# Fetching q and k as bfloat16 in runs of 18 tokens, in a kernel of block-causal attention followed by a hash-routed MoE

## The chip, the core and the metric

The kernel runs on one core of one Trainium2 chip. The metric is the device time of one execution in microseconds; before the change its median over three runs is 338.91 us (338.58 to 340.65). A profile shows where that time goes; its span, from the first to the last instruction, is 334.5 us.

The core has five engines that run side by side and wait for each other through semaphores: TensorE (PE in the profile; its weight loads are PEld), VectorE (DVE), ScalarE (ACT), GpSimd (POOL, called Pool in the text) and SyncE (SP), which here only starts transfers. Transfers between the chip's memory (HBM) and the on-chip memory (SBUF) run on 16 DMA engines, whoever starts them. TensorE writes its results to a small memory of its own, PSUM, from which VectorE or ScalarE must copy them.

## What is computed

```python
# attention: batch 8, heads 8, 576 tokens, head size 64
scores = q @ k.T / sqrt(64)                 # per batch and head
scores = where(pos_i // 64 >= pos_j // 64, scores, -1e9)   # causal by blocks of 64 tokens
x      = softmax(scores) @ v                # -> x: 4608 tokens x 512
# routing: each token goes to one of 8 experts
expert = token_ids * 2654435761 % 8
# expert e, on its tokens only
out[tokens of e] = relu(x[tokens of e] @ w1[e]) @ w2[e]    # 512 -> 1024 -> 512
```

All inputs and the output are float32 in HBM.

## The kernel before

The kernel works on *pairs* of two heads of one batch: 32 pairs, `g = 4 * b + pr`. For each pair it needs q and k with the head size on the partitions, so it fetches them with the tokens on the partitions, casts them to bfloat16 and transposes them on TensorE. `m` is the head within a pair; the two heads lie in the two halves of the partitions.

```python
    def load_qk(b, h0=0, h1=H, rest=True, main=True, engs=None):
        # float32, tokens 4p..4p+3 of a head on partition p (q), 2p, 2p+1 of each half (k);
        # the last 64 tokens in transfers of their own
        ...
            if main and w == 0:
                eng.dma_start(
                    t[:, 4 * h0 : 4 * h1, :].rearrange("p (h c) d -> p h (c d)", c=4),
                    src[b, h0:h1, 0:512, :].rearrange("h (p c) d -> p h (c d)", c=4),
                )
        ...

    def cast_qk(b, which, r0=0, r1=NP, rest=True):
        ...
            nc.vector.tensor_copy(           # float32 -> bfloat16, two pairs per call
                dst[:, 8 * r0 : 8 * r1, :].rearrange("p (r c m) d -> p r m c d", c=4, m=2),
                src[:, 8 * r0 : 8 * r1, :].rearrange("p (r m c) d -> p r m c d", c=4, m=2),
            )
        if rest:
            nc.gpsimd.tensor_copy(dst[:, 32:36, :], src[:, 32:36, :])

    def T_pair(g):                            # eight 128x128 transposes, one copy
        ...
        tp = psT.tile([P, 2, 512], BF16, name="tp", tag="tp")     # psT has two buffers
        for w in range(2):
            for c in range(4):
                ...
                nc.tensor.transpose(out=o, in_=..., identity=identbf[:])   # L236
        nc.vector.tensor_copy(qk[:, pr, :, 0:512], tp[:])                  # L241
    # T_rest(b): four transposes and two small copies (L211, L217) for the last 64 tokens
```

The scores of a pair are made in three chunks. The block mask is added on TensorE by a product of two small constant tiles. ScalarE takes the exponential into `pt`, the product with v follows two pairs later, and VectorE divides by the row sums (`norm`).

```python
    def mm_pair(b, pr, ps, o0, kt, q0, n, first=False):                    # L248
        for m in range(2):
            rows = slice(64 * m, 64 * m + 64)
            nc.tensor.matmul(ps[:, m, o0 : o0 + n],
                lhsT=qk[rows, pr, 1, 128 * kt : 128 * kt + 128],
                rhs=qk[rows, pr, 0, q0 : q0 + n], start=first, stop=False)
    # mm_c: the same in 64x64 tiles (L260); mm_mask: the mask product (L270)
    # S_chunk: mm_pair, mm_mask, then nc.scalar.activation(..., ACT.Exp)   # L294
    # PV(g, m): O = pt.T @ v, 15 matmuls (L331, L336); psO has one buffer
    # norm(g): reciprocal (L348) and two multiplications into xs (L351)
    # cast_v: v to bfloat16, on Pool but for the first batch (L188 to L199)

    def write_x(b):
        eng = nc.sync if b < BA - 1 else nc.gpsimd        # BA = 6
        for t in range(NT):                               # queries are held permuted
            r0 = S * b + P * t
            eng.dma_start(
                x_dram[r0 : r0 + P, :].rearrange("(j c) d -> c j d", c=4), xs[:, t, :])
        eng.dma_start(x_dram[S * b + 512 : S * b + S, :], xs[0:64, NT, :])
```

The routing is worked out beside the attention: `place_a` and `place_b` turn token numbers into lists of rows, one batch of tokens per two pairs. The MoE gathers rows of `x_dram` by these lists (`gather_x`, an indirect transfer on Pool, L567), transposes them, and runs two matmul stages per expert. Tokens of batches 0 to 5 are gathered early (tiles 0 to GA), those of batches 6 and 7 when the attention is over.

```python
    for g in range(NPAIRS + 2):
        b, pr = divmod(g, NP)
        ... S_chunk(g, 0); PV(g - 2, 0); S_chunk(g, 1); PV(g - 2, 1); norm(g - 2); S_chunk(g, 2)
        ... T_pair(g + 2); cast_qk(b + 1, ...); T_rest(b + 1) at pr == 2
        ... place_a at steps 5, 7, .. 19; place_b at steps 8, 10, .. 22
        ... cast_v for pair g + 3
        if pr == 1 and b >= 1:
            write_x(b - 1)
        if pr == (1 if b == 0 else 0) and b + 2 < B:
            load_qk(b + 2)
            load_v(b + 2)
        if g in (25, 26):
            load_w1(g - 25)            # 2 MB of float32, cast to bfloat16 in the transfer, Pool
        if g == 29:
            load_w2(0)
        if g in (27, 28):
            gather_x(g - 27, 0, GA)
    ...
    gather_x(0, GA, G)
    gather_x(1, GA, G)
    load_w2(1)
    for e in range(2):
        transpose_x(e, 0, GA)          # L683, L684
        stage_a_part(e, 0, GA)         # x @ w1 and relu: L715, L719
    ... then the late tiles, stage_b(0) (h @ w2: L729, L734, L736) and experts 2 to 7
```

Of the kernel before, what the change touches and what calls it, by code (L numbers as in the profile page):

```python
# [7 lines left out]
ALU = mybir.AluOpType  # L8
# [11 lines left out]

B, H, S, D = 8, 8, 576, 64
E, DM, FF = 8, 512, 1024
N = B * S
NT = 4
# [13 lines left out]
def kernel(  # L38
# [62 lines left out]
    def load_qk(b, h0=0, h1=H, rest=True, main=True, engs=None):  # L101
        if b not in loaded:
            loaded[b] = [ld.tile([P, 36, D], F32, name="qf", tag="qf"),
                         ld.tile([P, 36, D], F32, name="kf", tag="kf"), None]
        for w, src in ((0, q), (1, k)):
            t = loaded[b][w]
            eng = engs[w] if engs else nc.sync
            if main and w == 0:
                eng.dma_start(
                    t[:, 4 * h0 : 4 * h1, :].rearrange("p (h c) d -> p h (c d)", c=4),  # L110
                    src[b, h0:h1, 0:512, :].rearrange("h (p c) d -> p h (c d)", c=4),
                )
            elif main:
                for r in range(2):
                    eng.dma_start(
                        t[:, 4 * h0 : 4 * h1, :].rearrange(
                            "p (h r c) d -> p h r (c d)", r=2, c=2)[:, :, r],
                        src[b, h0:h1, 256 * r : 256 * r + 256, :].rearrange("h (p c) d -> p h (c d)", c=2),
                    )
            if rest:  # L120
                for g in range(2):
                    eng.dma_start(
                        t[64 * g : 64 * g + 64, 32:36, :],
                        src[b, 4 * g : 4 * g + 4, 512:576, :].rearrange("h r d -> r h d"),
                    )

    def load_v(b):
# [7 lines left out]
        for m in range(2):  # L135
            nc.sync.dma_start(
                vf[64 * m : 64 * m + 64, 32:36, :],
                v[b, :, 512:576, :].rearrange("(r m) s d -> m s r d", m=2)[m],
            )
        loaded[b][2] = vf  # L140

    casted = {}
# [24 lines left out]
    def cast_qk(b, which, r0=0, r1=NP, rest=True):  # L167
        src = loaded[b][which]
        cb = casted.setdefault(b, {})
        if which not in cb:  # L170
            cb[which] = att.tile([P, 36, D], BF16, name="qb" if which == 0 else "kb",
                                 tag="qb" if which == 0 else "kb")
        dst = cb[which]
        if r1 > r0:
            nc.vector.tensor_copy(
                dst[:, 8 * r0 : 8 * r1, :].rearrange("p (r c m) d -> p r m c d", c=4, m=2),
                src[:, 8 * r0 : 8 * r1, :].rearrange("p (r m c) d -> p r m c d", c=4, m=2),
            )
        if rest:
            nc.gpsimd.tensor_copy(dst[:, 32:36, :], src[:, 32:36, :])  # L180

    def cast_v(b, pr):
        vf = loaded[b][2]
        vx, v4 = vexts[b % 2]
        hs = slice(2 * pr, 2 * pr + 2)
        vm = vf[:, 0:32, :].rearrange("p (h s) d -> p h s d", h=H)
        eng = nc.vector if b == 0 and pr < 2 else nc.gpsimd
        eng.tensor_copy(vx[:, hs, 0:4, 0:D], vm[:, hs])  # L188
        if pr % 2:
            return  # L190
        hs = slice(2 * pr, 2 * pr + 4)
        nc.gpsimd.tensor_copy(vx[0:64, hs, 4:6, 0:D], vm[0:64, hs, 0::2, :])
        nc.gpsimd.tensor_copy(vx[64:128, hs, 4:6, 0:D], vm[0:64, hs, 1::2, :])

    def cast_v4(b):
        vf = loaded[b][2]
# [8 lines left out]
    def T_rest(b):  # L205
        qk = qkTs[b]
        tp = psT.tile([P, 8, P], BF16, name="tp", tag="tp")
        for w in range(2):
            src = casted[b][w]
            for x in range(2):  # L210
                nc.tensor.transpose(  # L211
                    out=tp[:, 2 * w + x, :],
                    in_=src[:, 32 + 2 * x : 34 + 2 * x, :].rearrange("p a d -> p (a d)"),
                    identity=identbf[:],
                )
        for w in range(2):
            nc.vector.tensor_copy(  # L217
                qk[:, :, w, 512:576].rearrange("p (g x) r -> p x g r", g=2),
                tp[:, 2 * w : 2 * w + 2, :].rearrange("p x (g r) -> p x g r", g=2),
            )  # L220

    def T_pair(g):
        b, pr = divmod(g, NP)
        if pr == 0:
            qkTs[b] = att.tile([P, NP, 2, S], BF16, name="qkT", tag="qkT")
        qk = qkTs[b]
        tp = psT.tile([P, 2, 512], BF16, name="tp", tag="tp")
        for w in range(2):
            src = casted[b][w]
            for c in range(4):  # L230
                s0 = (pr * 4 + c) * 2
                if w == 0:
                    o = tp[:, 0, :].rearrange("p (i c j) -> p c i j", i=4, c=4)[:, c]
                else:
                    o = tp[:, 1, 128 * c : 128 * c + 128]
                nc.tensor.transpose(  # L236
                    out=o,
# [610 lines left out]
```

## Time and profile before

| Engine | busy us | share of the span | instructions |
|---|---|---|---|
| TensorE (PE) | 276.5 | 83% | 3247 |
| TensorE weight loads (PEld) | 198.3 | 59% | 3247 |
| VectorE (DVE) | 152.5 | 46% | 342 |
| ScalarE (ACT) | 142.5 | 43% | 169 |
| Pool (POOL) | 183.4 | 55% | 265 |

| DMA queue | packets | MB | share of 16 engines |
|---|---|---|---|
| started by Pool (software) | 9248 | 32.73 | 41.1% |
| started by SyncE (hardware) | 55104 | 30.12 | 33.7% |
| started by ScalarE (hardware) | 2656 | 1.18 | 1.4% |

Busy times are sums over the whole span, and the phases of this kernel have different limits, so the totals decide nothing by themselves. TensorE's matmuls are pipelined and their ends are modelled, so a TensorE that shows as busy need not be working at its peak. Read the timeline to see which engine waits for which: an instruction that had to wait carries the idle time before it and the releaser, in brackets. The profile also states the granted TensorE clock, as a part of full speed; its mean here is 0.951.

### The profile page before, as it was taken

What the parts mean: (1) busy time and instruction counts of PE and PEld (TensorE: products, weight loads), DVE (VectorE), ACT (ScalarE), POOL (GpSimd) and SP (SyncE); (2) the same over time, 40 slices, a digit from 0 to 9 for tenths busy, and PEclk for the clock granted to TensorE, in tenths of its full rate; (3) what the DMA queues carried; (4) which work ended last, traced back from release to release, by engine and by line L of the source; (5) the groups of instructions that cost most, each with busy time, mean ns of one, the idle gap of its engine ahead of it and who ended that gap; (6) DMA issues with size and microseconds to landing.
All of it is one profiled execution on the core that took longest, in us unless ns stands there. A gap on an engine that the chain in (4) does not pass through costs nothing. (4 is left out here: it accounts for less than half of the span.)

```text
span 334.5 us, 7914 instructions
## 1 busy us (share of the span) xinstructions
PE 276.5 (83%) x3247; PEld 198.3 (59%) x3247; DVE 152.5 (46%) x342; ACT 142.5 (43%) x169; POOL 183.4 (55%) x265
## 2 busy tenths in 40 slices
PE   1559898989799899458589899799897996999990
PEld 0337676767577676347476594665745845759430
DVE  6487899888878775221011413033141130240430
ACT  1337888779687978304322050330501402406000
POOL 2185867687966529682487517447175075051451
PEclk9999999999989999959869999999999898999996
DMA  7999997979897975969189998677786586537231
GB/s 195 283 290 282 261 289 203 262 199 285 203 297 203 294 197 123 205 182 184 55 179 231 180 232 221 177 138 229 151 174 187 111 177 187 109 121 148 94 135 45
DMA packets 67044, 64.54 MB, mean 193 GB/s; under 512 B 17218, under 2 KB 61060, under 8 KB 64960
## 3 DMA queue, kind: packets, MB, share of 16 engines
q0 software_dynamic: 9248, 32.73, 41.1%
q1 hardware_dynamic: 55104, 30.12, 33.7%
q10 hardware_dynamic: 2656, 1.18, 1.4%
q8 instruction: 26, 0.43, 0.5%
q14 instruction: 10, 0.08, 0.1%
HBM read 67.15 MB, written 15.20 MB: 246 GB/s over the span
## 5 line engine op out<-in xcount | busy, mean ns | idle before, releaser
L294 ACT ACTIVATE pt<-ps 128x1024 bf16<-128x1024 f32 x96 | 94.2, 1023 | 34.4 <-PE ps L270 34.2
L701 ACT ACTIVATE hT<-hp 128x640 bf16<-128x640 f32 x48 | 33.6, 704 | 95.4 <-PE hp L696 78.6
L729 PE MATMUL yp<-w2b,hT 128*128 128x512 bf16 x320 | 70.2, 379 | 0.0
L696 PE MATMUL hp<-xT,w1b 128*128 128x320 bf16 x384 | 57.4, 309 | 9.1 <-ACT hT L701 8.2
L736 POOL DMA_INDIRECT out_dram<-ysb,perm x40 | 39.8, 995 | 38.6 <-DVE ysb L734 30.0
L696 PEld LDWEIGHTS <-w1b 128*128 128x128 bf16 x384 | 52.9, 145 | 13.5 <-issue 10.2
L567 POOL DMA_INDIRECT xg<-x_dram,perm x40 | 40.8, 1020 | 23.6 <-issue 12.9
L734 DVE COPY ysb<-yp 128x512 f32<-128x512 f32 x40 | 27.7, 692 | 55.9 <-PE yp L729 49.7
L729 PEld LDWEIGHTS <-hT 128*128 128x128 bf16 x320 | 31.1, 98 | 36.2
L684 DVE COPY xT<-tpx 128x512 bf16<-128x512 bf16 x40 | 15.6, 421 | 77.4 <-PE tpx L683 75.6
L331 PE MATMUL O<-vx,pt 128*128 128x65 bf16 x896 | 41.0, 199 | 6.7 <-DVE xs L351 5.4
L331 PEld LDWEIGHTS <-pt 128*128 128x128 bf16 x896 | 33.4, 101 | 10.2 <-issue 5.2
L248 PE MATMUL ps<-qkT 64*128 64x64 bf16 (+2 forms) x384 | 36.2, 269 | 3.0 <-ACT pt L294 2.6
L351 DVE TENSOR_TENSOR xs<-O,rs 128x320 bf16<-128x320 f32 x64 | 28.4, 486 | 1.1
L270 PE MATMUL ps<-maskq,maskk 64*128 64x64 bf16 (+1 forms) x256 | 28.1, 213 | 0.0
L188 POOL CAST vx<-vf 128x512 bf16<-128x512 f32 x30 | 21.1, 707 | 9.2 <-DMA vf<-in_v_dram 5.5
L719 ACT ACTIVATE hT<-hp 128x768 bf16<-128x768 f32 (+1 forms) x16 | 11.3, 704 | 31.7 <-PE hp L715 29.9
L241 DVE COPY qkT<-tp 128x1024 bf16<-128x1024 bf16 x32 | 22.0, 687 | 5.3 <-PE tp L236 4.6
L715 PE MATMUL hp<-xT,w1b 128*128 128x384 bf16 (+1 forms) x128 | 21.9, 338 | 2.3 <-DVE xT L684 2.3
L555 POOL DMA_DIRECT2D w1b<-in_moe_w_dram x8 | 4.8, 596 | 33.7 <-PE tpx L683 33.7
L683 PE MATMUL tpx<-identbf,xg 128*128 128x128 bf16 x160 | 14.7, 229 | 10.3 <-DMA xg<-x_dram,perm 6.6
L715 PEld LDWEIGHTS <-w1b 128*128 128x128 bf16 x128 | 17.4, 149 | 6.5 <-issue 2.9
(120 smaller groups left out, 289.6 us busy)
## 6 DMA issues: line engine op xcount, KB each, us to landing
vf<-in_v_dram SPq DMA_DIRECT2D x16, 512.0 KB, 5.9
w1b<-in_moe_w_dram POOLq DMA_DIRECT2D x8, 1024.0 KB
w2b<-in_moe_w_dram POOLq DMA_DIRECT2D x8, 1024.0 KB
qf<-in_q_dram SPq DMA_DIRECT2D x7, 1024.0 KB, 8.4
kf<-in_k_dram SPq DMA_DIRECT2D x14, 512.0 KB, 7.2
x_dram<-xs SPq DMA_DIRECT2D x20, 128.0 KB
x_dram<-xs POOLq DMA_DIRECT2D x12, 128.0 KB
qf<-in_q_dram SPq DMA_DIRECT2D x16, 64.0 KB, 6.3
```

Source lines behind the costliest of these rows:

```text
L248: nc.tensor.matmul(ps[:, m, o0 : o0 + n], lhsT=qk[rows, pr, 1, 128 * kt : 128 * kt + 128], rhs=qk[rows, pr, 0, q0 : q0 + n], start=first, ...
L270: nc.tensor.matmul(ps[:, m, o0 : o0 + 128 * n].rearrange("p (t h j) -> p t h j", h=2, j=16)[:, :, 0, :], lhsT=maskk[rows, c, :], rhs=maskq ...
L294: nc.scalar.activation(ptv[:, :, 512 * ch : 512 * ch + 512], ps[:], ACT.Exp, scale=SCALE)
L331: nc.tensor.matmul(O[:, t, :], lhsT=pt[:, m * PTW + o0 : m * PTW + o0 + 128], rhs=vx[:, h, i, :], start=(n == 0), stop=(n == t),)
L351: nc.vector.tensor_tensor(out=xs[:, :, 0:DM].rearrange("p t (d h k) -> p h t d k", d=4, h=H)[:, h], in0=O[:, m, :, 0:D].rearrange("p t (k ...
L567: nc.gpsimd.indirect_dma_start(out=xgs[g % (2 * G)][:], out_offset=None, in_=x_dram[0:n, :], in_offset=bass.IndirectOffsetOnAxis(ap=perm3[ ...
L696: nc.tensor.matmul(hp[:, t, 0:HC], lhsT=w1b[:, db, ft::NFT], rhs=xT[:, db, t * HC : (t + 1) * HC], start=(db == 0), stop=(db == NKT - 1),)
L701: nc.scalar.activation(hT[:, ft, :].rearrange("p (t n) -> p t n", t=2), hp[:, :, 0:HC], ACT.Relu)
L715: nc.tensor.matmul(hp[:, ft - f0, 0 : P * (t1 - t0)], lhsT=w1b[:, db, ft::NFT], rhs=xT[:, db, c], start=(db == 0), stop=(db == NKT - 1),)
L729: nc.tensor.matmul(yp[:], lhsT=hT[:, ft, tt * P : (tt + 1) * P], rhs=w2b[:, ft, :], start=(ft == 0), stop=(ft == NFT - 1),)
L734: nc.vector.tensor_copy(ysb[:], yp[:])
L736: ins = nc.gpsimd.indirect_dma_start(out=out[:, :], out_offset=bass.IndirectOffsetOnAxis(ap=perm3[:, gg : gg + 1], axis=0), in_=ysb[:], in ...
```

## The change

q and k are fetched by Pool and cast to bfloat16 in the transfer, so that no engine casts them. One transfer each per batch replaces several: partition `32 * h + j` holds the tokens 18 j to 18 j + 17 of head h, and, in a second slot, those of head h + 4. A run of 18 tokens is 4608 bytes in a row in HBM. Pairs are now the heads h and h + 4. A transpose takes one token of each run: 128 partitions (four heads, 32 runs) by 64 elements, and the two slots go to the two column halves of TensorE. The result is copied from PSUM with a stride, which puts queries in their natural order; keys are held in two sets, even and odd tokens. The mask product is in natural order as well. Rows of x then leave in their natural order, by two transfers per batch instead of five, and the routing needs no permutation.

Along with it the schedule moves: the transposes of a batch are five groups laid over the steps of the batch before it, q and k are requested at fixed steps with three buffers, the weights of the first two experts are all fetched inside the attention, and the output tiles have 8 buffers instead of 10.

```diff
+RUN = 18
+HS = S // 2
-    def load_qk(b, h0=0, h1=H, rest=True, main=True, engs=None):
-        ...                                          # cut
+    def load_qk(b):
+        loaded[b] = []
+        for w, src in ((1, k), (0, q)):
+            t = ld.tile([P, 2, RUN, D], BF16, name="qb" if w == 0 else "kb",
+                        tag="qb" if w == 0 else "kb", bufs=3)
+            nc.gpsimd.dma_start(
+                t[:].rearrange("p m c d -> p m (c d)"),
+                src[b].rearrange("(m h) (j c) d -> (h j) m (c d)", m=2, c=RUN))
+            loaded[b].insert(0, t)
+
+    load_qk(0)
...
-    def cast_qk(b, which, r0=0, r1=NP, rest=True):   # cut: all casts of q and k
-    def T_rest(b):                                   # cut
-    def T_pair(g):                                   # cut
+    def T_group(b, n, act=False):
+        ...
+        qd = qT[:].rearrange("p r (j c) -> p c (r j)", c=RUN)
+        kd = kT[:].rearrange("p x r (j c) -> p x c (r j)", c=RUN // 2)
+        tp = psT.tile([P, 8, P], BF16, name="tp", tag="tp")
+        copy = nc.scalar.copy if act else nc.vector.tensor_copy
+
+        def T(w, c, o):
+            for m in range(2):
+                nc.tensor.transpose(out=tp[64 * m : 64 * m + 64, o, :],
+                                    in_=loaded[b][w][:, m, c, :], identity=identbf[:])
+
+        if n < 4:
+            for c in range(8):
+                T(n // 2, 8 * n + c if n < 2 else 2 * c + n - 2, c)
+            copy(qd[:, 8 * n : 8 * n + 8] if n < 2 else kd[:, n - 2, 0:8], tp[:])
+        else:
+            for z in range(4):
+                T(z // 2, 16 + z % 2, z)
+            copy(qd[:, 16:18], tp[:, 0:2])
+            copy(kd[:, :, 8], tp[:, 2:4])
...
     def S_rest(b):
+        kR = att.tile([P, NP, 64], BF16, name="kR", tag="kR")
+        nc.vector.tensor_copy(kR[:].rearrange("p r (u x) -> p x r u", x=2), qkTs[b][1][:, :, :, 256:288])
...
     def write_x(b):
-        for t in range(NT):
-            r0 = S * b + P * t
-            eng.dma_start(
-                x_dram[r0 : r0 + P, :].rearrange("(j c) d -> c j d", c=4), xs[:, t, :])
+        eng.dma_start(
+            x_dram[S * b : S * b + 512, :].rearrange("(t p) d -> p t d", p=P), xs[:, 0:NT, :])
         eng.dma_start(x_dram[S * b + 512 : S * b + S, :], xs[0:64, NT, :])
...
-    load_qk(0, 0, 2, rest=False, engs=both)          # cut: q and k of batches 0 and 1 in pieces
+    for n in (2, 3, 0, 1, 4):
+        T_group(0, n, act=n in (1, 3))
+    Ts = {g: [] for g in range(NPAIRS + 2)}
+    for b in range(1, B):
+        at = {1: (2, 2, 3, 3, 3), 2: (5, 6, 6, 7, 7), 3: (8, 9, 10, 10, 10)}.get(
+            b, tuple(4 * b - 5 + z for z in (0, 1, 2, 3, 3)))
+        for n in range(5):
+            Ts[at[n]].append((b, n))
+    qk_at = {1: 2, 5: 3, 8: 4, 11: 5, 14: 6, 17: 7}
...
         if g == 0:
             cast_v(0, 0)
+            load_qk(1)
             cast_v4(0)
...
+        if g in qk_at:
+            load_qk(qk_at[g])
-        if g in (25, 26):
-            load_w1(g - 25)
-        if g == 29:
-            load_w2(0)
-        if g in (27, 28):
-            gather_x(g - 27, 0, GA)
+        if g in (22, 24):
+            load_w1((g - 22) // 2)
+        if g in (26, 30):
+            load_w2((g - 26) // 4)
+        if g in (28, 29):
+            gather_x(g - 28, 0, GA)
...
-    mo = ctx.enter_context(tc.tile_pool(name="mo", bufs=10))
+    mo = ctx.enter_context(tc.tile_pool(name="mo", bufs=8))
...
-    load_w2(1)                                       # after the attention
```

## The prediction

> **What bounds the kernel now.** I read the engine totals first, then the span in slices, then cut the span where the kernel's phases change and asked for the busy time of each engine in each stretch. A pair is two heads of one batch; there are 32, numbered from 0, and pair 0's first score matmul starts at 11.40 us, pair 1's at 18.85, pair 2's at 24.60, pair 3's at 29.54 (timeline). The stretches below begin and end with the normalisation of a pair, then with MoE stages. Columns: stretch, its length, then busy us and instruction count of each engine, the granted TensorE clock, the DMA share and GB/s.
>
> ```profile
> 31.84:61.30 29.46, 26.49 (x560) 20.20 (x554) 26.93 (x61) 23.83 (x27) 23.53 (x42) 1.00 1.01 260
> 61.30:107.54 46.24, 42.56 (x862) 32.34 (x862) 39.07 (x82) 36.01 (x40) 33.99 (x55) 0.96 0.87 238
> 107.54:135.31 27.77, 25.54 (x544) 19.13 (x544) 18.52 (x42) 23.76 (x27) 15.90 (x27) 1.00 0.76 202
> 135.31:146.00 10.69, 3.51 (x76) 2.95 (x73) 3.33 (x9) 1.76 (x2) 7.66 (x9) 0.79 0.97 230
> 146.00:178.40 32.40, 25.83 (x169) 20.62 (x170) 4.01 (x10) 10.45 (x15) 19.00 (x23) 0.81 0.67 140
> 178.40:200.68 22.28, 20.58 (x147) 15.03 (x145) 6.76 (x14) 6.45 (x10) 10.45 (x12) 1.00 0.95 215
> ```
>
> The reader is to see four phases. From 31.84 to 107.54 (norm of pair 1 to norm of pair 21, so 20 pairs at 3.79 us) VectorE is nearly full: 26.93 of 29.46 us in the first of the two rows. From 107.54 to 135.31 (8 pairs at 3.47) it is not, and TensorE with 25.54 of 27.77 is. From 135.31 to 146.00 TensorE works 3.5 of 10.7 us: it waits. From 146.00 to 178.40 the first two experts are started at a clock of 0.81 with holes. After that an expert takes a steady 21.8 us, which this change does not touch.
>
> How VectorE makes TensorE wait in the second stretch is read in the timeline (start, duration, engine, instruction, in brackets the idle time before it and its releaser): TensorE has issued the last transposes at 87.57 and cannot write the next PSUM buffer until a copy far back in VectorE's queue is done.
>
> ```profile
> 87.57 0.28 PE L211 MATMUL tp<-identbf,kb 128*128 128x128 bf16 x2
> 89.57 0.57 PE L518 MATMUL pq<-ohg,ohp 128*128 128x144 bf16 x5 [1.73 <-DVE qkT L241]
> ```
>
> The entry to the MoE, same view: the gather of the late tokens waits 10 us for the last rows of x to land, and TensorE for the gather.
>
> ```profile
> 145.88 2.10 POOL L362 DMA_DIRECT2D x_dram<-xs  x3 [1.06 <-DMA w1b<-in_moe_w_dram]
> 148.53 0.61 POOL L560 DMA_DIRECT2D w2b<-in_moe_w_dram  x1
> 162.81 1.09 POOL L567 DMA_INDIRECT xg<-x_dram,perm  x1 [10.09 <-DMA x_dram<-xs]
> 165.66 0.61 PE L683 MATMUL tpx<-identbf,xg 128*128 128x128 bf16 x4 [3.18 <-DMA xg<-x_dram,perm]
> ```
>
> The rows by shape of 31.84 to 107.54 give VectorE's price list (busy us, mean ns):
>
> ```profile
> L241 DVE COPY qkT<-tp 128x1024 bf16<-128x1024 bf16 x20 | 13.7, 686 | 1.2 <-PE tp L236 0.7
> L175 DVE CAST kb<-kf 128x1024 bf16<-128x1024 f32 x10 | 8.9, 886 | 0.0
> L175 DVE CAST qb<-qf 128x1024 bf16<-128x1024 f32 x10 | 7.9, 786 | 0.0
> L217 DVE COPY qkT<-tp 128x256 bf16<-128x256 bf16 x10 | 2.4, 280 | 0.0
> ```
>
> **What the Trainium skill says.** "VectorE: DVE Perf Modes", section "What auto-detection actually checks": the mode that packs two 16-bit values needs every tensor at a step of one element. The trace agrees for dense copies: 256 elements take 280 ns and 1024 take 686, so 0.53 ns each on top of 144 ns fixed, while the fp32 copy at L734 (512 in 692 ns) comes to (692 - 144)/512 = 1.07 ns. No run yet shows a strided bf16 copy. "DMA: Bandwidth & Descriptors", section "SWDGE vs HWDGE vs iDMA": a cast during a transfer must be issued from GpSimd; the weight loads here do so (about 0.6 us of Pool each). "TensorEngine Tiling (Array Packing)", sections "Key Properties" and "Restrictions": tiles work in parallel, a change of mode drains the array, and column tiling gives up the fast weight load. The 64x64 tiles of L260 agree with the first (below); nothing here shows the others. "TensorE: Matmul & The Clock Gate", Part 1: the clock is granted at half after idle time; the trace has 0.50 from 142 to 150 us, right after the holes.
>
> **The change, part by part.**
>
> *VectorE.* Removed per batch: two casts each of k and q, 2 x 0.886 + 2 x 0.786 = 3.34 us; four dense copies 4 x 0.686 = 2.74; two small ones 2 x 0.28 = 0.56. Sum 6.65. Added: four 128x1024 copies whose destination now steps by 18 (q) or 9 (k) elements. I take one element a pass for them: 0.144 + 1024 x 1.07 ns = 1.24 us each, 4.96; two of 256 elements at 0.42, 0.84; the gather kR, 256 elements, 0.35 (between the two rates). Sum 6.15. So VectorE gains only 0.5 us per batch, 0.12 per pair: the work of the casts comes back as strided copies. Norm (2 x 0.486 + 0.213 per pair) and the placing of tokens (0.964 + 0.546 + 0.292 per batch of tokens) stay. Pool gains a little, since its eight pairs of small casts (L180) go. Over 20 pairs: -2.5 us.
>
> *TensorE.* Per batch 36 transposes of 128x128 become 72 of 128x64, two at a time into the two column halves. Full ones run at about 58 ns start to start (four of L236 span 0.40 us, the last 0.226 of it). Eight 64x64 matmuls of L260 take 0.24 us from their start (86.60) to the next line's (86.84), 30 ns each. At that pace a pair of halves costs 60 ns, so 72 x 30 = 2.2 us per batch as before: 0. If each half waits for its own weights it could be 120 ns per pair, 4.3 us, +2.1 per batch.
>
> *DMA.* HWDGE moved 30.12 MB in 33.7% of the span (112.7 us of all 16 engines): 267 GB/s, so q and k of a batch, 2.36 MB, take 8.8 us. Casting weight loads from 134 to 142 us filled the engines at 199 to 217 GB/s of bf16 written; 1.18 MB at 210 is 5.6 us. Saved: 3.2 us of all engines per batch where they were full (share 1.01). The waits this removes are small: VectorE waited 3.3 us for q and k after 107 us, Pool 3.2 (L180). With more even TensorE work and no such waits I put the 8 pairs after 107.54 at 3.2 us instead of 3.47: -2.2.
>
> *Start.* Before, q and k arrive in pieces and pairs 1 to 3 wait; pair 3 starts at 29.54. After, all of k, then q, must land before pair 0. 2 us of issue, 5.6 us of transfer, shared with v, so landing near 9 to 13; about 3.5 us for the last three groups of transposes with copies (two on ScalarE); pair 0 at about 14. Then pairs 1 and 2 need no transposes and take some 3.2 us each; batch 1's q, issued on Pool only behind the v cast, may hold pair 3 to about 24. Gain 5, uncertain by 4; I count -4.
>
> *Entry to the MoE.* x is written by two transfers per batch, not five: on Pool three batches at 5 issues each (0.7 us, so 3.5 per batch) become about 1.4. Pool no longer stops on the cast of k at 119.84, so x of batch 5 is written when pair 23 is normalised, not 11 us later, and gathers don't hold up the last v cast. Both first w1 and w2 are fetched inside the attention (steps 22 to 30), so nothing large stands ahead of the last rows of x: they land in about 3 us instead of 10. From the last attention matmul at 143.2 to the first output matmul at 178.4 are 35.2 us. Its work at full clock is 32 x (0.160 + 0.107) us for each of two experts, 17.1, with 40 transposes at 0.06 and four copy lags near 0.6: 22 us. I expect 24 to 26: -10. The end of the attention, 7.9 us from norm 29 to 143.2 for what takes 4 to 5: -3.
>
> Sum: -2.5 + 0 - 2.2 - 4 - 10 - 3 = -21.7. Taken off 338.9 this is 317; since such gains partly meet new waits I say **319 us**.
>
> **Rivals.** (1) *VectorE gets worse*: strided writes cost more than 1.07 ns, or groups of two or three in one step pile up before two PSUM buffers. For it: two groups, or three, share a step (batch 1 at step 3, every batch at its third pair), and VectorE is the bound there. At 1.6 us per copy the 20 pairs lose 7 us; the total would be about 327. (2) *TensorE gets worse*: 120 ns per pair of halves adds 15 us over seven batches, part hidden under VectorE's bound; about 329. The 30 ns of L260 speaks against it, but those used four tiles. (3) *Pool and its queue become the path*: q, k, weights, x and gathers now share one queue in order, so weights may delay a batch's q or the x rows. q and k are asked for 3 to 4 pairs ahead (10 us or more against 6 to 8 us to land), which speaks against it; if it held, the entry gain halves, about 325. (4) *The start gets worse*, if v takes half the engines: pair 0 near 20 us, +3 rather than -4, about 326.
>
> **Range and chances.** One rival leaves 325 to 329; two together 331 to 336. If none holds and the entry is clean, 310. So 308 to 333, faster by over 2% (below 332.1) at 0.81, within 2% at 0.14, slower at 0.05.
>
> **What would show it.** In the profile after: copies into qT and kT near 1.24 us (right) or above 1.5 (rival 1); transposes of 128x64 whose group of 16 takes about 0.5 us (right) or 1 (rival 2); pair 0 at 12 to 16 us and pair 3 by 26; from 30 to 105 us about 3.65 us per pair with VectorE still above 85%; last x rows landing within 5 us of their issue, first output matmul within 27 us of the attention's end, clock near 1.0 between. The prediction is wrong if the pair time in the middle changes by over 0.3 us either way, or if the entry keeps its holes.

## The result and the profile after

The changed kernel takes **449.44 us** (448.83 to 450.28), the kernel before 338.97 beside it: ratio **1.325**, interval 1.320 to 1.330. I had predicted 319 us with a range to 333. The change makes the kernel slower by a third.

The totals of each engine and the span in slices, from the page of the kernel after:

```profile
PE 302.2 (68%) x3535; PEld 218.6 (49%) x3535; DVE 254.1 (57%) x310; ACT 154.2 (35%) x171; POOL 179.1 (40%) x284
...
DVE  1868959969879889889888322122404140404041
...
PEclk9999557559588578668866667999999999999997
```

VectorE has over 80% in most of the first 22 slices, the attention, and the TensorE clock lies mostly between 0.5 and 0.8 from the fifth to the 24th. Cut at the norms of pair 0, pair 22 and pair 31 and at the first output copy, with columns as in the prediction's first fence:

```profile
35.21:222.80 187.59, 101.99 (x1820) 75.45 (x1818) 164.79 (x143) 69.32 (x73) 67.04 (x130) 0.70 0.45 98
222.80:266.36 43.56, 31.59 (x538) 23.36 (x538) 25.73 (x36) 21.82 (x23) 14.29 (x21) 0.67 0.39 94
266.36:296.18 29.82, 25.72 (x178) 20.38 (x179) 5.02 (x13) 11.26 (x16) 15.29 (x17) 0.86 0.34 83
```

The same three stretches of the kernel before:

```profile
27.77:111.66 83.89, 77.24 (x1584) 58.55 (x1583) 73.46 (x159) 66.40 (x73) 63.87 (x105) 0.98 0.93 252
111.66:143.86 32.20, 24.93 (x526) 19.02 (x523) 16.81 (x40) 21.85 (x24) 18.60 (x27) 0.96 0.81 194
143.86:180.32 36.46, 27.75 (x177) 21.49 (x178) 5.12 (x13) 11.27 (x16) 21.46 (x27) 0.80 0.69 152
```

So the first 22 pairs more than double (VectorE busy 164.79 us, before 73.46), the next nine lose 11.4 us, and the entry to the MoE gains 6.6. DMA is no longer pressed: share 0.45 against 0.93 in the first stretch.

The price list of VectorE, rows by shape of about the first stretch (35 to 217 us):

```profile
L203 DVE COPY kT<-tp 128x1024 bf16<-128x1024 bf16 x12 | 55.7, 4700 | 0.0
L203 DVE COPY qT<-tp 128x1024 bf16<-128x1024 bf16 x12 | 54.6, 4577 | 7.8 <-PE tp L197 7.6
L208 DVE COPY kT<-tp 128x256 bf16<-128x256 bf16 x6 | 9.0, 1492 | 0.0
L207 DVE COPY qT<-tp 128x256 bf16<-128x256 bf16 x6 | 8.8, 1464 | 0.0
L267 DVE COPY kR<-kT 128x256 bf16<-128x256 bf16 x5 | 3.3, 667 | 0.0
```

Here is the miss: 4.6 to 4.7 us for a copy that I put at 1.24. What it does to TensorE is seen in the timeline of the kernel after, where batch 1 has three groups of transposes in one step (TensorE and VectorE alone; only rows that matter are left):

```profile
36.74 8.94 DVE L203 COPY qT<-tp 128x1024 bf16<-128x1024 bf16 x2 [0.39 <-PE tp L197]
...
39.45 0.23 PE L238 MATMUL ps<-maskq,maskk 64*128 64x128 bf16 x2
41.35 0.64 PE L197 MATMUL tp<-identbf,kb 128*64 128x128 bf16 x16 [1.68 <-DVE qT L203]
...
45.73 1.07 PE L197 MATMUL tp<-identbf,kb 128*64 128x128 bf16 x16 [3.74 <-DVE qT L203]
...
46.96 9.13 DVE L203 COPY kT<-tp 128x1024 bf16<-128x1024 bf16 x2
51.66 0.43 PE L197 MATMUL tp<-identbf,qb 128*64 128x128 bf16 x4 [4.86 <-DVE kT L203]
...
58.35 0.61 PE L216 MATMUL ps<-qT,kT 64*128 64x448 bf16 x4 [6.05 <-DVE kT L208]
```

From 39.7 to 58.35 us TensorE does 2.3 us of transposes and waits for the rest: each group needs one of two PSUM buffers, a buffer comes free only when a copy of 4.6 us is done, and the next batch's scores stand behind all of it in TensorE's order. The 16 half-width transposes take 0.64 us at full clock and 1.07 at half.

At the start and the entry, the timeline of the kernel after has:

```profile
9.69 1.92 PE L197 MATMUL tp<-identbf,kb 128*64 128x128 bf16 x32 [9.69 <-DMA kb<-in_k_dram]
10.79 4.63 DVE L203 COPY kT<-tp 128x1024 bf16<-128x1024 bf16 x1 [6.31 <-PE tp L197]
11.64 4.65 ACT L203 COPY kT<-tp 128x1024 bf16<-128x1024 bf16 x1 [9.45 <-PE tp L197]
...
25.37 0.61 PE L216 MATMUL ps<-qT,kT 64*128 64x448 bf16 x4
...
272.13 1.08 POOL L526 DMA_INDIRECT xg<-x_dram,perm  x1 [3.00 <-DMA x_dram<-xs]
```

ScalarE pays the same price, so helping with it doesn't help. The wait for the last rows of x has fallen from 10.09 to 3.00 us, as foreseen.

### The profile page after: what moved, and what is told of

It reads as the page before. It is cut to its first block, busy times and chain, and to the rows that moved or that the text cites. A ratio compares the mean times of both kernels' runs of the same rounds, so it can differ in the third digit from the quotient of the medians.

```text
span 447.1 us, 8380 instructions
## 1 busy us (share of the span) xinstructions
PE 302.2 (68%) x3535; PEld 218.6 (49%) x3535; DVE 254.1 (57%) x310; ACT 154.2 (35%) x171; POOL 179.1 (40%) x284
## 5 line engine op out<-in xcount | busy, mean ns | idle before, releaser
L203 DVE COPY qT<-tp 128x1024 bf16<-128x1024 bf16 x15 | 68.2, 4572 | 10.7 <-PE tp L197 10.5
L203 DVE COPY kT<-tp 128x1024 bf16<-128x1024 bf16 x15 | 69.7, 4693 | 6.3 <-PE tp L197 6.3
L216 PE MATMUL ps<-qT,kT 64*128 64x64 bf16 (+2 forms) x384 | 44.5, 319 | 20.6 <-DVE kT L208 13.1
L640 PEld LDWEIGHTS <-w1b 128*128 128x128 bf16 x384 | 52.2, 144 | 11.0 <-issue 10.1
L302 PE MATMUL O<-vx,pt 128*128 128x65 bf16 x896 | 51.3, 223 | 5.2 <-DVE xs L322 5.2
L302 PEld LDWEIGHTS <-pt 128*128 128x128 bf16 x896 | 42.6, 116 | 10.3 <-PE ps L238 3.4
L197 PE MATMUL tp<-identbf,qb 128*64 128x128 bf16 x288 | 16.1, 266 | 29.3 <-DVE kT L203 18.2
L197 PE MATMUL tp<-identbf,kb 128*64 128x128 bf16 x288 | 15.3, 252 | 19.8 <-DVE qT L203 10.1
L197 PEld LDWEIGHTS <-qb 128*64 128x64 bf16 x288 | 12.9, 137 | 31.5 <-issue 28.4
L216 PEld LDWEIGHTS <-kT 64*128 64x128 bf16 x384 | 13.9, 102 | 27.4 <-DVE kT L208 13.6
```

Of the source, the lines that this page charges most:

```text
L197: nc.tensor.transpose(out=tp[64 * m : 64 * m + 64, o, :], in_=loaded[b][w][:, m, c, :], identity=identbf[:])
L203: copy(qd[:, 8 * n : 8 * n + 8] if n < 2 else kd[:, n - 2, 0:8], tp[:])
L216: nc.tensor.matmul(ps[:, m, o0 : o0 + n], lhsT=kT[rows, x, pr, 128 * r : 128 * r + 128], rhs=qT[rows, pr, q0 : q0 + n], start=first, stop= ...
L302: nc.tensor.matmul(O[:, t, :], lhsT=pt[:, m * PTW + o0 : m * PTW + o0 + 128], rhs=vx[:, h, i, :], start=(n == 0), stop=(n == t),)
L640: nc.tensor.matmul(hp[:, t, 0:HC], lhsT=w1b[:, db, ft::NFT], rhs=xT[:, db, t * HC : (t + 1) * HC], start=(db == 0), stop=(db == NKT - 1),)
```

## The experiments

The sets of runs lay on different chips, and the kernel before took 326 us in three of them and 340 and 343 in the other two, so each ratio below is to the kernel before on the same chip. Medians in microseconds are of all runs of a kernel, while the ratios leave out those that fell into a slower state of the chip. Ratios don't carry from chip to chip to better than about 0.013: one kernel, with the routing first, gave 1.004 on one chip and 0.991 on another (its two runs are below). Its profiles show where: from norm 0 to norm 22 it took 96.32 and 94.58 us, from norm 22 to norm 31 31.40 and 26.32. So across sets I compare only the first of these stretches, and there differences below 2 us say nothing.

**A copy by itself.** No kernel of the case, but copies of 1024 elements per partition out of PSUM, one after the other, the destination stepping by 1, 2, 4, 8, 9, 16 and 18 elements; then runs of 8. The output is left zero.

```
+for n in (1, 2, 4, 8, 9, 16, 18): V(d[n], pb[:])            # L96, in this order
+V(r18, pb...)   # L97  runs of 8 at a step of 18, source dense
+V(r18, byc)     # L99  the same runs, source stepping by 128
+V(gs, byc)      # L100 destination dense, source stepping by 128
+V(d[1], src) ; V(d[18], src)   # L101, L102: the source in SBUF, destination dense and at a step of 18
+V(f4, pf) ; V(f4, sf)   # L105, L107: float32, 512 elements, step 4, from PSUM and from SBUF
+A(d[1], ...) ; A(d[4], ...) ; A(d[8], ...) ; A(d[18], ...)  # L110, ScalarE
```

> Copies alone, each form twice, no attention and no MoE (the output is left zero). Line theory: what costs is the write of single 2-byte elements that lie 16 bytes or more apart in SBUF. Then from PSUM on VectorE: dense 0.69 us for 1024 elements, step of 2 elements about 1.2, step 4 between 1.2 and 2.3, steps 8, 9, 16 and 18 all about 4.6; runs of 8 elements 0.7 to 1.3 whether the source is dense or stepping by 128; fp32 written at a step of 16 bytes about four times the dense copy; ScalarE the same ratios; an SBUF source written at a step of 18 also about 4.6. PSUM theory: what costs is the read of a bfloat16 PSUM buffer filled in another way; then a step of 18 here costs 1.2 us, from PSUM or SBUF.

The timeline of these copies on VectorE, second round:

```profile
87.45 0.66 DVE L96 COPY d<-pb 128x1024 bf16<-128x1024 bf16 x1
88.04 1.27 DVE L96 COPY d<-pb 128x1024 bf16<-128x1024 bf16 x1
89.21 2.39 DVE L96 COPY d<-pb 128x1024 bf16<-128x1024 bf16 x1
91.41 4.72 DVE L96 COPY d<-pb 128x1024 bf16<-128x1024 bf16 x1
95.74 4.85 DVE L96 COPY d<-pb 128x1024 bf16<-128x1024 bf16 x1
100.21 4.65 DVE L96 COPY d<-pb 128x1024 bf16<-128x1024 bf16 x1
104.49 4.74 DVE L96 COPY d<-pb 128x1024 bf16<-128x1024 bf16 x1
108.86 0.89 DVE L97 COPY r<-pb 128x1024 bf16<-128x1024 bf16 x1
...
110.32 1.20 DVE L99 COPY r<-pb 128x1024 bf16<-128x1024 bf16 x1
111.45 1.20 DVE L100 COPY gs<-pb 128x1024 bf16<-128x1024 bf16 x1
112.58 0.40 DVE L101 COPY d<-src 128x1024 bf16<-128x1024 bf16 x1
112.91 2.34 DVE L102 COPY d<-src 128x1024 bf16<-128x1024 bf16 x1
```

The time doubles with the step until 8 elements (16 bytes), then stays at 4.7 us: (4.65 - 0.14) / 1024 = 4.4 ns per element. Walking the *source* with a step costs 1.20 us, about the 1.24 I had taken for "strided". Runs of 8 whose starts lie 36 bytes apart cost 0.89, so it is not the gap: it is 2-byte writes that stand alone. Two expectations failed. Out of SBUF the write at a step of 18 took 2.34 us, where 4.6 was expected: six times its dense copy of 0.40, but half of what the same write takes out of PSUM. So the source counts as well, and the price of 4.4 ns holds for copies out of PSUM. And float32 at the same 16 bytes takes not four times the dense copy but 1.05 us for 512 elements from PSUM (dense 0.68 and 0.89 in the two rounds) and 0.60 from SBUF (dense 0.41), far less per write. ScalarE takes 2.47 us at a step of 4 and 4.81 and 4.89 at 8 and 18.

**The change with dense copies.** It leaves out the order of the tokens (scores are those of other tokens); the work is the same.

```diff
-            copy(qd[:, 8 * n : 8 * n + 8] if n < 2 else kd[:, n - 2, 0:8], tp[:])
+            copy(qf[:, 1024 * n : 1024 * n + 1024] if n < 2 else kf[:, n - 2, 0:1024],
+                 tp[:].rearrange("p c a -> p (c a)"))
```

> The kernel after with one thing changed: the copies of transposed q and k write densely, so the order of tokens in qT and kT is wrong while every count of work is the same. Line theory: copies of 1024 elements at 0.69 us, VectorE's load per batch 6.15 us less 4 x 0.55 less 2 x 0.14, and the whole at 312 to 322 us, since the rest of my prediction stands. Theory that the rest of the change also costs (Pool's queue, transposes in halves, late loads): copies at 0.69 but the whole at 340 or more. PSUM theory: copies still near 4.6 us and the whole near 449.

Measured: 324.89 us, ratio 0.993 (0.990 to 0.997), copies at 0.69 us, norm 0 to norm 22 in 94.94 us instead of 187.59. So the steps of the destination are nearly the whole loss. But the gain I had promised, 6%, isn't there either, although a copy now costs less than I had counted. Something else took it; the timeline of the dense kernel names it:

```profile
52.49 0.81 DVE L270 COPY kR<-kT 128x256 bf16<-128x256 bf16 x1
...
53.36 0.31 PE L275 MATMUL ps<-qT,kR 64*64 64x64 bf16 x8 [1.35 <-DVE kR L270]
...
57.33 1.06 PE L197 MATMUL tp<-identbf,qb 128*64 128x128 bf16 x16 [3.65 <-DMA qb<-in_q_dram]
58.51 0.69 DVE L205 COPY qT<-tp 128x1024 bf16<-128x1024 bf16 x1 [5.20 <-PE tp L197]
```

Two new waits: the gather kR is issued only when TensorE is about to need it, behind a norm on VectorE; and q of a batch lands late, because Pool asks for k and q behind its casts. After the second wait TensorE runs at half clock (1.06 us for 16 transposes).

**The same bytes, walked the other way.** The destination runs over 8 neighbouring tokens first, and the step goes to the source. The output is the reference's.

```diff
-            copy(qd[:, 8 * n : 8 * n + 8] if n < 2 else kd[:, n - 2, 0:8], tp[:])
+            copy(qi[:, :, 8 * n : 8 * n + 8] if n < 2 else ki[:, n - 2, :, 0:8],
+                 tp[:].rearrange("p c a -> p a c"))
```

> The kernel after with the same copies walked in another order: 8 neighbouring tokens innermost, so that each 16 bytes of the destination are written in one go, while the PSUM source is read at a step of 128 elements. Results as in the kernel after. Line theory, if only writes pay: 0.7 to 1.3 us per copy and the whole at 315 to 325 us. If reads of PSUM at a wide step pay as the writes do: 4.6 us per copy and the whole near 449.

Measured: 336.43 us, ratio 1.028 (1.021 to 1.034); a copy takes 1.22 us. One edit of the order in which a copy is walked takes back 0.297 of the 0.325 (on another chip). It also gives almost exactly the price that I had assumed (1.24), so the rest of my sum can be tested on it: at that price it should have been 0.94.

**The kernel before with the same kind of step.** Its 32 copies write at a step of 16 elements (token order left out).

```diff
-        nc.vector.tensor_copy(qk[:, pr, :, 0:512], tp[:])
+        nc.vector.tensor_copy(qk[:, pr, :, 0:512].rearrange("p w (j c) -> p w c j", c=16),
+            tp[:].rearrange("p w (c j) -> p w c j", c=16))
```

> The kernel before with one thing added: its 32 copies of transposed q and k (1024 elements) write at a step of 16 elements (32 bytes), so the order of tokens is wrong while every count of work is the same. Line theory: each goes from 0.69 to about 4.5 us, VectorE's load per pair from 3.7 to 7.5 us in the middle of the attention, and the whole to 440 to 465 us, as slow as the kernel after or slower. Theory that the loss comes from other parts of the change: 339 to 360 us.

Measured: 417.22 us, ratio 1.276 (1.270 to 1.282). The page's row of that kernel:

```profile
L241 DVE COPY qkT<-tp 128x1024 bf16<-128x1024 bf16 x32 | 143.7, 4492 | 4.9 <-PE tp L236 4.9
```

Nothing else of the change is needed to lose a quarter. The whole is below the 440 to 465 us expected, of which some 12 us are the chip's (326 us for the kernel before, not 339). A side result: this kernel's entry to the MoE took 29.5 us with the old x transfers, probably because its slower attention left the weights and x time to land.

**The new waits.** On the copies in runs of 8: the gather kR right behind the batch's last copy; q and k asked for one or two steps earlier, q first; then both.

```diff
 (in T_group, n == 4)
             copy(kd[:, :, 8], tp[:, 2:4])
+            kRs[b] = att.tile([P, NP, 64], BF16, name="kR", tag="kR")
+            nc.vector.tensor_copy(kRs[b]..., kT[:, :, :, 256:288])
 (loads)
-    qk_at = {1: 2, 5: 3, 8: 4, 11: 5, 14: 6, 17: 7}
+    qk_at = {1: 2, 3: 3, 6: 4, 9: 5, 12: 6, 15: 7}
```

> Theory: with the copies walked in runs of 8 (ratio 1.028 to before), the attention is still longer than before's because the late-token scores stand in TensorE's order behind the kR gather, which VectorE does only after a norm and a placing; the row for that wait was 6.7 us in 5 waits, and the half clock after each costs about as much again. With the gather done right behind the last copy of the batch, one to two steps ahead, that wait should be gone, norm 0 to norm 31 should fall from 138.8 us to about 126, and the ratio from 1.028 to about 0.99. Rival: VectorE, busy 72 of 102 us there, is simply too slow with copies of 1.22 us and the wait moves to the next buffer; then the ratio stays within 0.01 of 1.028.

> Same copies in runs of 8; q and k are asked for one or two steps earlier, q first, ahead of Pool's other work of the step. Theory: late q is a second, smaller wait (1.3 us in one wait in that profile, 3.7 in the dense one), so the ratio falls from 1.028 to about 1.02. Rival: the queue of Pool is the true limit of the middle part (the rows that follow a late q are all late), and the ratio falls below 1.00. Second rival: asking earlier takes DMA time from v and the ratio rises.

> Both edits together on the copies in runs of 8. Theory: the two waits are separate, so the gains add: norm 0 to norm 31 about 122 us, ratio about 0.98, which would beat both kernels. Rival: once the kR wait is gone VectorE's queue sets the pace and the earlier loads bring nothing: ratio as with the gather alone. If both fail, the ratio stays at 1.02 to 1.03.

Measured: 1.019 (1.011 to 1.027), 1.021 (1.013 to 1.029) and 1.010 (1.007 to 1.014). On this one chip, norm 0 to norm 22 took 97.62, 103.13 and 97.15 us: with the loads early, the gather is worth 6 us; with the gather early, the loads are worth 0.5. The first theory is right in kind: the kR wait, 6.6 us in five waits with the loads alone, is gone. The 122 us that I expected to norm 31 were 131, but 33.93 of them lie behind norm 22, where the kernel that the expectation started from took 28.73 on its chip, so they don't test the size. What is left is a pile-up, in the timeline of the kernel with both edits:

```profile
33.02 1.08 PE L198 MATMUL tp<-identbf,kb 128*64 128x128 bf16 x32
...
33.87 2.35 DVE L206 COPY kT<-tp 128x1024 bf16<-128x1024 bf16 x2
35.14 0.30 PE L198 MATMUL tp<-identbf,qb 128*64 128x128 bf16 x4 [1.04 <-DVE kT L206]
...
36.46 1.27 DVE L212 COPY kT<-tp 128x256 bf16<-128x256 bf16 x1
...
37.79 0.39 PE L222 MATMUL ps<-qT,kT 64*128 64x448 bf16 x4 [2.23 <-DVE kT L212]
...
38.31 1.02 ACT L268 ACTIVATE pt<-ps 128x1024 bf16<-128x1024 f32 x1 [4.10 <-PE ps L244]
```

Three groups in one step, and the next scores wait for the last k tokens of the last one, whose copy of 256 elements still writes 2 bytes at a time and takes 1.27 us.

**The new weight times alone.** The kernel before with w1, w2 and the gathers at the steps of the change.

```diff
-        if g in (25, 26):
-            load_w1(g - 25)
+        if g in (22, 24):
+            load_w1((g - 22) // 2)
 (w2 and gathers likewise; load_w2(1) behind the attention is dropped)
```

> The kernel before with only the new weight and gather times (w1 at steps 22 and 24, w2 at 26 and 30, gathers at 28 and 29), x still written in five transfers a batch. Theory: the entry to the MoE (36.5 us from norm 31 to the first output copy, against 28.7 to 29.8 in every kernel with the change) shrinks because of when the weights are asked for, so this kernel has an entry of about 30 us and a ratio of 0.98. Rival: what shrank it are the single x transfers and the q and k taken off the queues; then the entry stays near 36 us and the ratio near 1.00, or above if the weights now hold up Pool's casts of v.

Measured: 1.017 (1.005 to 1.030). The theory falls: weights asked for earlier don't by themselves shorten the entry. The change's entry is shorter by something else it does at the end of the attention (two transfers of x instead of five, no q and k in the other queues); which of them was not separated. A slow attention isn't needed for it: in the dense spread kernel below the entry takes 29.69 us.

**Groups spread over five steps.** On the kernel with both edits; then the same with dense copies, the dense one without the spreading, and the first with the gather kR on Pool.

```diff
-        at = {1: (2, 2, 3, 3, 3), 2: (5, 6, 6, 7, 7), 3: (8, 9, 10, 10, 10)}.get(
-            b, tuple(4 * b - 5 + z for z in (0, 1, 2, 3, 3)))
+        at = {1: (1, 2, 2, 3, 3), 2: (4, 5, 5, 6, 6)}.get(
+            b, tuple(4 * b - 6 + z for z in range(5)))
```

> On the kernel with copies in runs of 8, the early gather and the early loads (ratio 1.0103): the five groups of transposes of a batch are given to five steps, one each, ending a step earlier, instead of four steps with two (batches 1 and 3: three) in the last. Theory: the last of two or three groups in one step waits for one of two PSUM buffers (1.0 to 1.2 us), then two or three copies stand one behind the other on VectorE (1.2 us each, 1.3 for the last k tokens), and the first scores of the next batch, next in TensorE's order, wait for the last of them (2.2 us at 37.8 us, ScalarE idle for 4.1). Spread, these waits go: norm 0 to norm 31 falls from 131 us to about 122, the ratio to about 0.985. Rival: VectorE has no time to give (about 13.6 us of work per batch of some 14.8), so the waits only move: ratio 1.00 to 1.01.

> The same with the copies written densely (the tokens then stand in the wrong order, so the scores are those of other tokens; the amount of work is that of the change). It is the change without the price of its strides and without its pile-ups. If both together explain the whole miss, it should give what I predicted and a little more, since a dense copy costs 0.69 us where I counted 1.24: ratio 0.92 to 0.94. If there is a third cost (half-width transposes, Pool's queue, the start), it stays at 0.96 or above. The dense kernel without these moves had 0.9934.

> Dense copies, early gather and early loads, but the groups still two or three to a step. It divides the gain of the kernel beside it: if pile-ups cost even when a copy takes only 0.69 us, this one lies about 0.02 above it (0.95 to 0.97); if pile-ups matter only because copies are slow, the two lie within 0.005 of each other.

> The first of these four with the gather of the late k tokens (0.3 to 0.7 us a batch) on Pool instead of VectorE. Theory that VectorE sets the pace in the first 22 pairs: it gains about 0.4 us a batch, 0.01 of the ratio at most. Rival: Pool, which shares its queue with the casts of v and with the loads, does it late and TensorE waits for it: ratio up by 0.01 or more.

Measured: 0.988 (0.980 to 0.995), **0.957** (0.950 to 0.965), 0.966 (0.956 to 0.975) and 0.997 (0.994 to 1.000). Norm 0 to norm 22 in the dense kernels: 94.94 us with the change's order, 85.36 with gather and loads early, 83.35 spread too. So the order cost the dense kernel 9.6 us for the late gather and loads and 2.0 for the pile-ups (the last two kernels ran on one chip: 314.28 and 312.49 us). The 0.957 is above the 0.92 to 0.94 expected. The dense spread kernel in the stretches to norm 22, norm 31 and the first output copy:

```profile
29.07:112.42 83.35, 77.99 (x1822) 59.33 (x1820) 60.93 (x145) 66.83 (x72) 65.88 (x129) 1.00 0.90 200
112.42:139.62 27.20, 23.27 (x524) 17.85 (x522) 12.06 (x33) 21.83 (x24) 15.83 (x25) 0.96 0.82 192
139.62:169.31 29.69, 25.58 (x178) 20.39 (x179) 5.02 (x13) 11.26 (x16) 15.29 (x17) 0.86 0.43 102
```

VectorE has dropped to 60.93 of 83.35 us, yet the stretch is no shorter than before's 83.89: TensorE, 77.99 of 83.35 busy at full clock, has no time to give. It had little before, too: 77.24 of 83.89, more than VectorE. The gather on Pool brings nothing.

**The change's own copies in the mended order.**

```diff
-            copy(qi[:, :, 8 * n : 8 * n + 8] if n < 2 else ki[:, n - 2, :, 0:8],
-                 tp[:].rearrange("p c a -> p a c"))
+            copy(qd[:, 8 * n : 8 * n + 8] if n < 2 else kd[:, n - 2, 0:8], tp[:])
```

> The change's own strided copies (4.6 us each) with all three mendings of the order: early gather, early loads, groups spread over five steps. Theory: the stride is the cost and needs no pile-up to hurt, since 4 x 4.6 + 2 x 1.4 us of copies with 6.6 us of norms and placing is some 28 us of VectorE a batch: norm 0 to norm 31 stays at 205 us or more and the ratio at 1.24 to 1.30 (the change itself: 1.325). Rival: most of the loss was the pile-up of slow copies in one step, and spreading frees it: ratio below 1.15.

Measured: 432.44 us, ratio 1.267 (1.254 to 1.279). Its first 22 pairs:

```profile
37.87:205.99 168.12, 108.96 (x1828) 80.18 (x1823) 163.43 (x145) 70.38 (x74) 65.11 (x127) 0.66 0.48 106
```

VectorE is busy 163.43 of 168.12 us. The change's order of groups, gather and loads cost 187.59 - 168.12 = 19.5 us. The dense kernel in the same order took 83.35, so 84.8 us are the bare price of the slow copies.

**The start.** On the kernel with copies in runs of 8, mended and spread: v of batch 1 asked for by ScalarE behind its first copies; v of batch 0 too; and the first part of the routing ahead of batch 0's transposes.

```diff
-    load_v(1)
 ...
+    load_v(1, nc.scalar)        # second kernel: load_v(0, nc.scalar) behind group n == 3 as well
 (third kernel)
+    next(rgen)
     for n in (2, 3, 0, 1, 4):
         T_group(0, n, act=n in (1, 3))
-    next(rgen)
```

> On the copies in runs of 8 with the mended order (ratio 0.9875), the v of batch 1 is asked for by ScalarE behind its first copies instead of at the start. Theory of the late start: k and q (landed at 9.6 and 13.0 us) share the engines with 4.7 MB of v, so without half of it q lands near 11 and the first scores, 19.3 us there, start 1.5 to 2 us earlier; the ratio falls by 0.005. Rival: the start is set by the chain behind the landing (copies, the routing's first part on VectorE), and nothing moves.

> Both first v asked for later, batch 0's behind ScalarE's first copy. Theory: k lands near 6 us and q near 8.5, first scores near 15, and the norm of pair 0 (30.2 us) near 27, unless v of batch 0 then comes late for its first PV. Rival: v late, norm of pair 0 at 30 or later, ratio up.

> The first part of the routing (on VectorE and five small matmuls) put ahead of batch 0's transposes, where VectorE is idle until 10.8 us anyway. Theory: TensorE's wait of 2.9 us for the routing at 18.9 us goes, the first scores start 1 to 2 us earlier, ratio down by 0.005. Rival: they then wait for the last k copy (done at 17.6) instead, and the gain is under 1 us.

Measured: 1.009 (1.005 to 1.013), 1.015 (1.002 to 1.027) and 1.004 (1.000 to 1.008). The kernel without these edits did not run on this chip, so its ratio of 0.988 can't be set beside these; only the starts can. Norm 0 fell at 29.55, 30.63 and 27.95 us, against 30.08 without these edits (the third of these kernels had 28.37 on the chip of that 30.08). With both v later, k lands at 7.21 us and q at 10.00 instead of 9.6 and 13.0, so v does hold them back; but then Pool gets its first v only at 19.81 us (13.75 without these edits), and nothing is won. The routing first is worth about 2 us at the start.

**The best version, side by side.** The spread kernel and the one with the routing first, once more.

> The kernel with copies in runs of 8, early gather, early loads and spread groups once more (0.9875 on the first chip), beside the one with the routing first, on one chip. If the 0.9875 is the kernel's, the ratio lies between 0.98 and 0.995 here; if it was that chip's, at 1.00 or above, since the kernel with the routing first gave 1.0039 on another.

> The same with the first part of the routing ahead of batch 0's transposes. Its profile had the norm of pair 0 2.2 us earlier (27.95 against 30.18) and that of pair 3 3.1 us earlier. If this start is worth what it looks, this kernel is 2 to 3 us (0.006 to 0.009 of the ratio) faster than the one beside it; if the time is given back later, the two are equal.

Measured on one chip: 325.46 us over all runs (323.9 over those of the ratio), 0.993 (0.990 to 0.996), and **323.11 us, 0.991** (0.988 to 0.995). The timelines show the start, first without the routing ahead, then with it:

```profile
19.26 0.41 PE L359 MATMUL pr<-identbf,eb 8*128 8x8 bf16 x5 [2.94 <-DVE et L362]
19.60 0.61 PE L222 MATMUL ps<-qT,kT 64*128 64x448 bf16 x4
```

```profile
5.72 0.40 PE L359 MATMUL pr<-identbf,eb 8*128 8x8 bf16 x5 [5.72 <-DVE et L362]
...
17.83 0.61 PE L222 MATMUL ps<-qT,kT 64*128 64x448 bf16 x4 [1.70 <-DVE kT L212]
```

The 2.94 us wait for the routing has become one of 1.70 for the last k copy. The second version beats the kernel before by 0.9% and the change by a quarter; between the two versions the intervals overlap. Norm 0 to norm 22 takes 95.89 and 94.58 us: spreading gained only 1.3 us on the 97.15 of the walked copies, less than the 1.7 us by which one kernel differed between two chips, so no gain of the spreading is shown here; the rival named there (the waits only move) fits as well. In the second, VectorE is busy 78.80 us and TensorE 82.21 of 94.58: neither is full. Against the 83.35 us of dense copies TensorE idles 12.4 us instead of 5.4 (8.1 of them until a copy of k on VectorE is done, 3.9 until Pool is) and is busy 4.2 us longer, at a clock of 0.93 instead of 1.00. How to close that gap is open.

## Why the prediction was wrong

Terms as the prediction summed them, against the kernel before; on the right the dense spread kernel, the change without its price for strides and with a mended order. Each is the difference of the stretches above (start: norm 0, 27.77 us before). The right column sets two chips against each other, which makes its third row and its sum uncertain by some 5 us; on its own chip that kernel is 14.3 us faster than the kernel before.

| term | predicted us | the change | dense, mended |
|---|---|---|---|
| start | -4 | +7.4 | +1.3 |
| first 22 pairs (VectorE, TensorE) | -2.5 + 0 | +103.7 | -0.5 |
| last 9 pairs (DMA, end of attention) | -2.2 - 3 | +11.4 | -5.0 |
| entry to the MoE | -10 | -6.6 | -6.8 |
| sum | -21.7 | +115.9 | -11.0 |

**VectorE: the step that failed**, "I take one element a pass for them: 0.144 + 1024 x 1.07 ns = 1.24 us each". Measured: 4 x 4.63 + 1.46 + 1.49 + 0.67 = 22.1 us per batch where I had 6.15. Of the +103.7 us, 91.3 are VectorE's added busy time (164.79 - 73.46), and 12.4 its added idle time. The 1.07 ns came from a float32 copy with neighbouring elements and was carried to 2-byte elements far apart. I had written that no run yet showed a strided bf16 copy, and went on with an unmeasured price for the engine that sets the pace. "VectorE: DVE Perf Modes", section "What auto-detection actually checks", says that steps lose the packed mode; true, but that is the smaller loss (0.66 to 1.27 us at step 2, about the price that I had taken). I had left aside the note on lines in "SBUF — State Buffer", section "Door 1: The DMA port swizzle": a line has 16 bytes, each new one pays a penalty unless it is hit at least twice, and bf16 may stride by up to 8 for free. The price levels off at just 16 bytes, which fits the line. Three things don't fit, and there the measurement decides: a step of 4, two elements to a line, costs 2.39 us, nearly twice what the lost packing alone costs at step 2; float32 alone on a line costs far less; and the same lone writes cost half when the source is SBUF. The mechanism was not shown; the price was.

**Rival 1** named this very case, "strided writes cost more than 1.07 ns, or groups of two or three in one step pile up before two PSUM buffers". Both halves came true. I gave it 1.6 us per copy and 7 us in all; it was 4.6 and over 100. A rival whose size nobody has measured has no upper end, and my range gave it one.

**TensorE, right.** 16 half-width transposes in 0.64 us, 30 ns apart after the first: nothing lost; rival 2 didn't happen. But I had read VectorE as the bound of the 20 pairs, when the rows of the prediction show TensorE as full (26.49 of 29.46 us, then 42.56 of 46.24 against VectorE's 39.07), and its waits from norm 0 to norm 22 before sum to 6.7 of 83.89 us. So a lighter VectorE had little to give: even at 0.69 us a copy, with VectorE 12.5 us less busy, this term gives -0.5. I had counted VectorE's saved time as time of the stretch.

**DMA and the last pairs, not settled.** The -5.0 of the dense kernel looks like the -5.2 of both terms, but it sets two chips against each other. With copies in runs of 8 these nine pairs took 26.3 to 28.7 us on two chips and 31.4 to 34.4 on the two where the kernel before takes 340 and 343 us, against 32.20 before on a chip where it takes 339. So no gain is shown on chips of that kind. Rival 3 held in a small way: one late q of 3.65 us in the dense kernel; loads one or two steps earlier were worth 0.5 us once the gather was early. The wait that I missed was **kR**: I priced it (0.35 us) but did not ask where it stands. It is issued in front of its user, behind a norm; moved, it gave 6 us.

**Start, wrong sign.** I had pair 0 at about 14 us. Even at 0.69 us a copy it is at 18.5, for k is complete only at 9.6 and q at 13.0 (in my range of 9 to 13), then come the copies, and TensorE's next instruction is the routing's, which waits 1.8 us for VectorE (2.9 where the copies are walked). Rival 4, +3, was right in kind.

**Entry, right in direction, two thirds in size.** First output matmul 27.9 us after the last product with v (266.3 to 294.2), before 35.2, predicted 24 to 26. Its work I had summed at full clock; the row of that stretch has a clock of 0.86 and TensorE busy for 25.7 us. Why it shortened is settled only in part: the gather waits 3.0 us for x instead of 10.1, and the weight times alone don't do it.

## What to carry to other kernels

Before an engine that sets the pace is given a copy, ask how many bytes it writes side by side: out of PSUM, 2-byte elements that stand alone cost seven times the dense copy, and the same bytes walked so that the step falls on the source cost 1.8 times. Measure that one instruction first; it decides more than all other terms together. And for each small instruction added, look where it stands in its engine's order, not only at its duration: a gather of 0.6 us in front of its user cost 6 us. Last, a relieved engine gains nothing where another is as full: here TensorE was.

## What the runs showed of the hardware that was not expected

- Copies of bf16 from PSUM to SBUF, written at a step of 1, 2, 4, 8 and 18 elements took 0.66, 1.27, 2.39, 4.72 and 4.74 us per 1024 on VectorE; at 4, 8 and 18 ScalarE took 2.47, 4.81 and 4.89. Reading PSUM at a step of 128 elements took 1.20. From SBUF on VectorE, dense and at a step of 18, it was 0.40 and 2.34.
- 256 elements at a step of 9 elements took 1.27 us in the attention, three times the same count in pairs of neighbours (0.41).
- A stop of TensorE can be paid twice: in the changed kernel 16 transposes after a wait of 1.68 us took 0.64 us at a granted clock of 1.00, and 16 after the next wait, of 3.74 us, took 1.07 at 0.50.
